# Other work in quarter units, on both sides of the probability products: a fused attention and long-convolution kernel

## The chip, the cores and the metric

The kernel runs on one core of a Trainium2 chip. The metric is device time in microseconds for one launch. Before the change the median of three runs is 1089.19 us (1088.64 to 1089.75).

## What is computed

Two independent layers on inputs of 2048 positions and 512 channels; their outputs stand side by side. The first is attention with 32 query heads of width 16 that share one key and one value head. The second is a gated long convolution, written with a Fourier transform.

```python
def _A_ref(x, wq, wk, wv, wo):            # x 1 x 2048 x 512, H = 32, Dh = 16
    q = (x @ wq).reshape(B, S, H, Dh).transpose(0, 2, 1, 3)
    k, v = x @ wk, x @ wv
    p = softmax(einsum("bhqd,bkd->bhqk", q, k) * Dh ** -0.5)
    o = einsum("bhqk,bkd->bhqd", p, v)
    return o.transpose(0, 2, 1, 3).reshape(B, S, H * Dh) @ wo

def _B_ref(q, k, v, shift_k, ssm_k, ssm_D):
    k_shift = causal convolution of k with shift_k, 4 taps
    kv = k_shift * v
    y = irfft(rfft(kv padded to 2 S) * rfft(ssm_k padded))[:S] + kv * ssm_D
    return q * y

out = concatenate([_A_ref(...), _B_ref(...)], axis=-1)
```

## The kernel before

**Attention.** A block is 512 queries of four heads, in two pairs, against 16 tiles of 128 keys. There are 32 such blocks (`NQ`) of 16 key tiles, two score tiles for each, so 1024 score tiles of 128 x 1024. For each of them TensorE makes two score matmuls (L699, `scores`), in float16 with 49 rows; ScalarE takes the exponential of the tile (L707); and TensorE multiplies half of the probabilities of two tiles with the values (L719, `pv`): four column-tiled products of 32 columns, 256 results wide, in float32, which stand as eight records in the trace. The value products of a block are summed in one PSUM bank, the accumulator (`self.acc`); at a block's end VectorE copies it out (L729).

**Turns.** `attend` (L735) writes the order out by hand. A turn issues three score tiles and their exponentials, then three value products of the turn before, then "other work" by `fill.step` (L755). If the accumulator changes inside a turn (`full`), the other work goes ahead of the first product of the new accumulator (L752). Three PSUM tiles hold scores, so the score matmul of a turn needs the exponential of the same place in the turn before. Two more banks (pool `pf`, L96) hold the accumulator and everything else that TensorE does: one bank for the other work at a time, besides the moments when the accumulator changes. 1024 score tiles in threes make 342 turns.

**Other work.** Six threads, Python generators, yield before each piece what it costs on TensorE and on VectorE:

- `rest_of_q` (L647): the query projection, 14 banks of 512 columns, each a sum of four products, cut by VectorE and stored; after each a bound for the softmax's shift (`bound`, L572); and at the end `flag` (L680), which reduces all bounds to one flag with a VectorE reduction, a TensorE transposition (L686) and two more VectorE operations.
- `conv_pe` (L388): the convolution's transforms. `forward` (L198, two products of 256 columns per bank, 16 banks for the short and 16 for the long transform of each of two channel blocks), `long_forward` with transposes ahead (L255), `backward` (L347, 16 banks of four products of 256 columns).
- `conv_short` (L413) and `conv_dve` (L429): VectorE alone, the four taps and the short Fourier steps and products between the transforms (L134 and others). `conv_pe` waits for them: the second `long` for the product of block 0, `backward` of a block for its inverse steps.
- `wo_heads` (L782) and `wo_part` (L816): the normalized heads come back from memory in 15 groups of which each needs a fixed step and some 15 steps of waiting, and a group's buffer (five of them) comes free when its projection is done. The output projection takes them in sets: groups 0 to 3, 4 to 7, 8 to 11, then 12 and 13, then 14, and the last block separately (L857 and `last`, L872).

`_Fill` (L894) hands them out. Each step adds a budget to two credits, TensorE's and VectorE's, capped (L919). Threads are asked in order; the one that `hurry` (L641) names comes first. A piece is issued when TensorE's credit covers it within a slack of 60, a VectorE piece while that credit is positive. Only one new piece per step, apart from those that continue the same bank (`HOLD`, the holder); while a bank is open no other thread may use TensorE. At the last turn `finish` (L945) issues whatever is left, ahead of the last value products.

A piece is a product 256 columns wide and costs 460 by the planner, a bound 350, a set of four transposes 500. A product (`mm`, L193) is four column-tiled matmuls, which become two passes with a weight load for each.

```python
RATE = 740.0, 2500.0        # added per turn: TensorE, VectorE
MOST = 1400.0, 2900.0       # caps
SLACK = 60.0
```

Of the kernel before, what the change touches and what calls it, by code (L numbers as in the profile page):

```python
# [39 lines left out]

RATE = 740.0, 2500.0
MOST = 1400.0, 2900.0
SLACK = 60.0
WO_AT = 290, 370, 440
OB = 5

# [34 lines left out]


WAIT = -1.0
HOLD = True


class _Emit:  # L90
# [18 lines left out]

    def wide(self):  # L110
        return self.ps.tile([P, 2, 512], F32, tag="s", name=self.nm("x"))

# [78 lines left out]
    def mm(self, out, w, x, start=True, stop=True):  # L193

        for j in range(0, P, 32):
            self.nc.tensor.matmul(out[j : j + 32], w[:, j : j + 32], x, start=start, stop=stop)  # L196

    def forward(self, src, c, m, ft):  # L198

        for q in range(2):  # L200
            yield (920 / 2, 700) if q else (920 / 2, 0, HOLD)
            if not q:
                b = self.bank()
            self.mm(b[:, q * CB : (q + 1) * CB], ft[:, q, :], src)
        self.nc.vector.tensor_copy(c[:, :, m, :], b.rearrange("p (q n) -> p q n", q=2))  # L205

    def table(self, n, m2):
        t = self.w.tile([P, 2, 2, P], F32, tag="ft", bufs=FT, name=self.nm(n))
# [6 lines left out]
    def conv_load(self):  # L215
        nc, I, w = self.nc, self.I, self.w
        self.dt = self.c.tile([P, 4], F32, name="dt")
        nc.sync.dma_start(self.dt, I["B_ssm_D"].rearrange("(c p) -> p c", p=P))
        sk = self.c.tile([P, 4, 4], F32, name="sk")
        nc.sync.dma_start(sk, I["B_shift_k"].rearrange("(c p) t -> p c t", p=P))  # L220
        yield WAIT, 6
        yield 240, 600
        tp = self.bank()
        for ct in range(4):
            nc.tensor.transpose(tp[0:4, ct * P : (ct + 1) * P], sk[:, ct, :], self.ident)
        tps = w.tile([4, 512], F32, tag="s2", bufs=S2, name="tps")
        nc.vector.tensor_copy(tps, tp[0:4, :])
        self.skd = self.dr.tile([4, 512], F32, name="skd")
        nc.sync.dma_start(self.skd, tps)
        rows = lambda t: t.rearrange("b (p m) c -> (b p) m c", m=16)  # L230
        self.kr, self.vr, self.qr, self.orr = rows(I["B_k"]), rows(I["B_v"]), rows(I["B_q"]), rows(self.out)
# [10 lines left out]
    def long_forward(self, blk, hin, ch):  # L242
# [14 lines left out]
            nc.vector.tensor_copy(hT[m], b.rearrange("p (i n) -> p i n", i=2))  # L257

        for m in (0, 2):
            yield 500, 700  # L260
            turn(m)
        for m in range(0, 16, 2):
            if m < 12:
                ft[m // 2 + 2] = self.table("ff", m // 2 + 2)
                yield 500, 700
                turn(m + 4)
            for i in range(2):
                yield from self.forward(hT[m][:, i, :], ch, m + i, ft[m // 2][:, i])
# [78 lines left out]
    def backward(self, blk, cx, places):  # L347
# [15 lines left out]
        for m2 in range(8):  # L363
            if m2 < 6:
                load(m2 + 2)
            if m2 == 7:
                self.seen.add(("b", blk))
            r = self.s2("r")
            for i in range(2):
                m = 2 * m2 + i  # L370
                for cc in range(2):
                    yield (920 / 2, 700) if i == cc == 1 else (920 / 2, 0, HOLD)
                    if i == cc == 0:
                        b = self.bank()
                    self.mm(
                        b[:, i * CB : (i + 1) * CB],
                        ft[m2][:, i, cc, :],
                        cx[:, cc, 4 * g2[m // 4] + g1[m % 4], :],
                        start=cc == 0,
                        stop=cc == 1,  # L380
                    )
            nc.vector.tensor_tensor(r, b.rearrange("p (i n) -> p i n", i=2), q[m2], ALU.mult)  # L382
            nc.gpsimd.dma_start(self.orr[:, 2 * m2 : 2 * m2 + 2, D + blk * CB : D + (blk + 1) * CB], r)  # L383

    def spectrum(self):
# [166 lines left out]
        nc.vector.tensor_scalar(self.wb[:, 8:16], blk[:, 0:8], cut, None, ALU.mult)  # L552
        nc.vector.tensor_scalar(self.gm[:, 16:17], kmr, cut, None, ALU.mult)

    def q_mm(self, g, c, b, dk, cols=slice(0, 512)):
        self.mm(b[:, cols], self.wq[g][:, dk, :], self.xT[c][:, dk, cols], start=dk == 0, stop=dk == 3)

    def q_out(self, g, c, b):

# [87 lines left out]
    def rest_of_q(self):  # L647
        for c in range(4):
            self.qc = c
            for g in range(4):  # L650
                if c == g == 0:
                    continue
                if c or g > 1:
                    b = None
                    for n in range(8):
                        yield (920 / 2, 0, HOLD) if n < 7 else (920 / 2, 2600)
                        b = b or self.bank()
                        self.q_mm(g, c, b, n % 4, slice(n // 4 * 256, n // 4 * 256 + 256))
                    self.q_out(g, c, b)
                yield WAIT, 2  # L660
                yield 350, 1100
                self.bound(g, c, self.bank())
            self.seen.add(f"q{c}")
            if c < 2:
                self.xT[c + 2] = self.w.tile([P, 4, 512], F32, tag="xt", bufs=2, name=f"xT{c + 2}")
                self.nc.sync.dma_start(self.xT[c + 2], self.xd[c])
        self.qc = 4
        self.flag()

    def stack(self, n, rows=KR):  # L670

# [8 lines left out]
    def flag(self):  # L680

        nc = self.nc
        g1 = self.c.tile([P, 1], F32, name="g1")
        nc.vector.tensor_reduce(g1, self.gm, AX.X, ALU.max)
        b = self.bank()
        nc.tensor.transpose(b[0:1, 0:P], g1, self.ident)  # L686
        g2 = self.c.tile([1, 1], F32, name="g2m")
# [47 lines left out]
    def attend(self, fill):  # L735
        self.od = self.dr.tile([NQ, P, 512], F32, name="od")
        x, steps = 0, NQ * NKT
        for u in range(3, 2 * steps + 3, 3):
# [7 lines left out]
            if u >= 2 * steps:  # L746
                fill.finish()

            full = [y for y in range(x + 1, end) if y % (2 * NKT) == 0]
            for y in range(x, end):  # L750
                if y in full:
                    fill.step(self.step)  # L752
                self.pv(y)
            if not full:
                fill.step(self.step)  # L755
            x = end
        self.last()

# [39 lines left out]

    def wo_rows(self, i, groups):

        b = None
        for h in range(2):
            cols = slice(256 * h, 256 * h + 256)
            for G in groups:
                yield (920 / 2, 700) if h and G == groups[-1] else (920 / 2, 0, HOLD)
                b = b or self.bank()
                self.mm(
                    b[:, cols],
                    self.oc[G][:, i * P : (i + 1) * P],
                    self.wo[G % 4][:, cols],  # L810
                    start=G == groups[0],
                    stop=G == groups[-1],
                )
        return b

    def wo_part(self):  # L816
        nc, w, I = self.nc, self.w, self.I
# [30 lines left out]
            yield 0, 1800  # L848
            self.over(self.ao, t, h)
        for i in range(4):  # L850
            b = yield from self.wo_rows(i, range(14, 15))
            nc.vector.tensor_tensor(self.wp[i], self.wp[i], b, ALU.add)
        for i in range(4):
            yield 920, 700
            b = self.bank()
            self.mm(b, t[:, 2, i * P : (i + 1) * P], self.wl[0])
            nc.vector.tensor_tensor(self.wp[i], self.wp[i], b, ALU.add)  # L857

    def over(self, a, t, h):

# [33 lines left out]
class _Fill:  # L894
# [3 lines left out]
    def __init__(self, threads, hurry):  # L898
# [2 lines left out]
        self.credit = [0.0, 0.0]  # L901
        self.holder = None

    def ask(self, t, i):

        while t[0] is not None and t[2] <= i:
            if t[1] is None:
                t[1] = next(t[0], None)
                if t[1] is None:
                    t[0] = None  # L910
                    return None
            if t[1][0] != WAIT:
                return t[1]
            t[2] = i + t[1][1]
            t[1] = None
        return None

    def step(self, i):
        c = self.credit = [min(c + r, m) for c, r, m in zip(self.credit, RATE, MOST)]  # L919
        once = True  # L920
        more = True
        while more:
            more = False
            first = self.hurry()
            for t in sorted(self.threads, key=lambda t: t is not self.threads[first or 0]):
                a = self.ask(t, i)
                if a is None:
                    continue
                if a[0] > 0:
                    if c[0] < a[0] - SLACK or not (once or self.holder is t) or self.holder not in (None, t):  # L930
                        continue
                    once = False
                    self.holder = t if len(a) > 2 else None
                elif c[1] <= 0:
                    continue
                c[0] -= a[0]
                c[1] -= a[1]
                t[1] = None
                t[1] = next(t[0], None)
                if t[1] is None:  # L940
                    t[0] = None
                more = True
                break

    def finish(self):  # L945
        while any(t[0] is not None for t in self.threads):
            for t in self.threads:
                if t[0] is None or self.holder not in (None, t):
                    continue
                if t[1] is None:  # L950
                    t[1] = next(t[0], None)
                if t[1] is None:
                    t[0] = self.holder = None
                else:
                    self.holder = t if len(t[1]) > 2 else None
                    t[1] = None
                    t[1] = next(t[0], None)
                    if t[1] is None:
                        t[0] = self.holder = None


def _general(tc, I, out):
# [149 lines left out]
```

## Time and profile before

| | us |
|---|---|
| median of three runs | 1089.19 |
| profiled execution | 1089.51 |
| its span, first to last instruction | 1087.7 |
| TensorE busy in matmuls | 1013.4 |
| ScalarE busy | 967.4 |
| VectorE busy | 610.4 |
| exponentials (L707), 1024 | 960.4 |
| value products (L719), 8192 records | 519.8 |
| score matmuls (L699), 2048 | 309.4 |

The mean granted clock of TensorE was 0.991. In the profile PE is TensorE's matmuls, PEld its weight loads (they overlap the matmuls), DVE is VectorE, ACT ScalarE, POOL GpSimd, SP SyncE; L196 is a line of the kernel, and since `mm` issues all products of the other work, they all stand under L196 and are told apart by their tiles (`f<-xT,wq` queries, `f<-a,ff`, `f<-hT,ff` and `f<-sp,fi` transforms, `f<-wo,o` and `f<-wl,lr` output projection). A group's row has its busy time, the mean duration of one in ns, then the idle time of the engine just before it and what ended that. A timeline row has its start, its duration (of a merged run of equal instructions), and in brackets the idle time before it. Matmul durations include the drain, which overlaps the next matmul, so costs are best read from start to start.

### The profile page before, as it was taken

What the parts mean: (1) busy time and instruction counts of PE and PEld (TensorE: products, weight loads), DVE (VectorE), ACT (ScalarE), POOL (GpSimd) and SP (SyncE); (2) the same over time, 40 slices, a digit from 0 to 9 for tenths busy, and PEclk for the clock granted to TensorE, in tenths of its full rate; (3) what the DMA queues carried; (4) which work ended last, traced back from release to release, by engine and by line L of the source; (5) the groups of instructions that cost most, each with busy time, mean ns of one, the idle gap of its engine ahead of it and who ended that gap; (6) DMA issues with size and microseconds to landing.
All of it is one profiled execution on the core that took longest, in us unless ns stands there. A gap on an engine that the chain in (4) does not pass through costs nothing.

```text
span 1087.7 us, 31787 instructions
## 1 busy us (share of the span) xinstructions
PE 1013.4 (93%) x13971; PEld 463.4 (43%) x13971; DVE 610.4 (56%) x825; ACT 967.4 (89%) x1032; POOL 96.3 (9%) x149
## 2 busy tenths in 40 slices
PE   7899999999999999999997999989988999998996
PEld 4344444444444444444443444434433444444442
DVE  3434774577577877786785356898789011000122
ACT  2798989999999999999997889999999999999993
POOL 2004210000000000013022021000000120000000
PEclk9899999999999999999999999999999999999999
DMA  6417433311211110113234243201011341110101
GB/s 218 147 48 229 131 136 140 102 53 56 110 54 44 54 54 26 43 57 125 63 119 131 84 139 117 70 29 39 29 49 40 97 136 41 38 39 28 49 2 42
DMA packets 47548, 87.30 MB, mean 80 GB/s; under 512 B 11132, under 2 KB 26026, under 8 KB 46380
## 3 DMA queue, kind: packets, MB, share of 16 engines
q1 hardware_dynamic: 33996, 43.50, 12.4%
q0 software_dynamic: 11648, 40.89, 11.6%
q8 instruction: 111, 1.82, 0.7%
q10 hardware_dynamic: 1760, 0.81, 0.3%
q14 instruction: 33, 0.27, 0.1%
HBM read 60.16 MB, written 25.02 MB: 78 GB/s over the span
## 4 chain that ended last, share of the span: by engine, by line
PE 66%; ACT 18%; issue 9%; DVE 4%; DMA 2%; POOL 0%; ACTq 0%; DVEq 0%; POOLq 0%
PE f L719 31%; PE s L699 18%; ACT p L707 18%; PE f L196 14%; PE f L255 1%; DMA xc<-in_A_x 1%; DMA kk<-in_B_k 1%; DVE ao L729 1%; DMA skd<-tps 1%; DMA wkv<-in_A_wk 1%; DVE t L312 0%; PE x L480 0%; DVE sp L134 0%; PE f L497 0%; DVE kc L515 0%
## 5 line engine op out<-in xcount | busy, mean ns | idle before, releaser
L707 ACT ACTIVATE p<-s 128x1024 f32<-128x1024 f32 x1024 | 960.4, 1069 | 84.3 <-PE s L699 76.7
L719 PE MATMUL f<-p,vx 128*32 128x256 f32 x8192 | 519.8, 385 | 5.4 <-DVE ao L729 5.3
L699 PE MATMUL s<-st,kst 49*128 49x512 f16 x2048 | 309.4, 382 | 41.4 <-ACT p L707 39.8
L719 PEld LDWEIGHTS f<-p,vx 128*32 128x32 f32 x8192 | 230.4, 110 | 234.1 <-issue 106.9
L699 PEld LDWEIGHTS <-kst 49*128 49x128 f16 x2048 | 97.3, 94 | 262.2 <-issue 219.2
L134 DVE TENSOR_TENSOR sp<-sp 128x1024 f32<-128x1024 f32 x96 | 111.6, 1213 | 0.0
L205 DVE COPY sp<-f 128x512 f32<-128x512 f32 x64 | 44.1, 689 | 76.0 <-PE f L196 75.7
L196 PE MATMUL f<-xT,wq 128*32 128x256 f32 (+1 forms) x960 | 67.8, 394 | 1.2 <-DVE gm L589 1.2
L729 DVE COPY ao<-f 128x512 f32<-128x512 f32 x31 | 21.4, 690 | 79.4 <-PE f L719 79.4
L196 PE MATMUL f<-wo,o 128*32 128x256 f32 x960 | 65.0, 379 | 0.0
L134 DVE TENSOR_TENSOR sp<-sp,sp 128x1024 f32<-128x1024 f32 x48 | 56.3, 1219 | 0.3
L824 DVE COPY wp<-f 128x512 f32<-128x512 f32 x12 | 8.3, 692 | 76.6 <-PE f L196 76.6
L382 DVE TENSOR_TENSOR r<-f,q 128x512 f32<-128x512 f32 x16 | 11.1, 692 | 65.7 <-PE f L196 65.7
L562 DVE TENSOR_SCALAR cut<-f 128x512 f32<-128x512 f32 x16 | 11.1, 691 | 64.2 <-PE f L196 64.0
L209 POOL DMA_DIRECT2D ff<-in_ff x32 | 17.6, 551 | 281.9 <-PE s L699 252.4
L196 PEld LDWEIGHTS f<-xT,wq 128*32 128x32 f32 x960 | 31.1, 110 | 23.3 <-issue 3.8
L196 PEld LDWEIGHTS f<-wo,o 128*32 128x32 f32 x960 | 31.2, 110 | 20.7 <-issue 0.2
L196 PE MATMUL f<-a,ff 128*32 128x256 f32 x512 | 34.5, 380 | 1.7 <-issue 0.9
L383 POOL DMA_DIRECT2D out<-r x16 | 11.6, 724 | 275.5 <-DVE r L382 252.0
L196 PE MATMUL f<-sp,fi 128*32 128x256 f32 x512 | 34.8, 379 | 0.0
L196 PE MATMUL f<-hT,ff 128*32 128x256 f32 x512 | 34.2, 379 | 0.0
L314 DVE TENSOR_TENSOR a<-a,t 128x512 f32<-128x512 f32 x48 | 33.1, 689 | 1.2
(106 smaller groups left out, 535.7 us busy)
## 6 DMA issues: line engine op xcount, KB each, us to landing
ff<-in_ff POOLq DMA_DIRECT2D x32, 256.0 KB, 4.2
od<-ao SPq DMA_DIRECT2D x30, 256.0 KB
kk<-in_B_k POOLq DMA_DIRECT2D x12, 640.0 KB, 4.7
qd<-qp SPq DMA_DIRECT2D x48, 128.0 KB
st<-qd SPq DMA_DIRECT2D x60, 98.0 KB
v<-in_B_v POOLq DMA_DIRECT2D x16, 256.0 KB, 4.5
hin<-in_B_ssm_k POOLq DMA_DIRECT2D x4, 1024.0 KB, 6.7
fi<-in_fi POOLq DMA_DIRECT2D x16, 256.0 KB, 3.8
```

The lines of the kernel that those rows point to most:

```text
L134: v.tensor_tensor(part(out), part(a), part(b), op)
L196: self.nc.tensor.matmul(out[j : j + 32], w[:, j : j + 32], x, start=start, stop=stop)
L205: self.nc.vector.tensor_copy(c[:, :, m, :], b.rearrange("p (q n) -> p q n", q=2))
L209: self.nc.gpsimd.dma_start(t, self.I[n][:, 2 * m2 : 2 * m2 + 2])
L314: nc.vector.tensor_tensor(a, a, t, ALU.add)
L382: nc.vector.tensor_tensor(r, b.rearrange("p (i n) -> p i n", i=2), q[m2], ALU.mult)
L383: nc.gpsimd.dma_start(self.orr[:, 2 * m2 : 2 * m2 + 2, D + blk * CB : D + (blk + 1) * CB], r)
L562: nc.vector.tensor_scalar(cut, b, LIM, -LIM, ALU.min, ALU.max)
L699: self.nc.tensor.matmul(s[:, e, :], self.kst[rows, k * P : (k + 1) * P], self.st[n][rows, pr, :], start=True, stop=True,)
L707: self.nc.scalar.activation(p, s, AF.Exp, scale=DH**-0.5 / SC / SC)
L719: nc.tensor.matmul(self.acc[32 * j : 32 * j + 32, cols], self.vx[:, k, :], self.pt[2 * i + j // 2][:, j % 2, cols], start=k == h == 0, sto ...
L729: nc.vector.tensor_copy(a, self.acc)
```

## The change

The unit of other work becomes a product's quarter, 128 columns, and both credits are counted in new sizes: 3 units a turn with a cap of 4, and 2300 for VectorE. A new generator `columns` offers what is left of a product and takes as many quarters as the credit covers, in one piece; pieces of different widths go into one bank, and only the first piece of a bank starts it. In a turn, `fill.turn` adds the budget; then, straight after the scores and ahead of the value products, `fill.step(self.step, False)` issues only pieces that continue an open bank; after the value products `fill.step(self.step, True)` may start a new bank, and issues VectorE's pieces. A turn with a change of accumulator has only the latter, at its old place. Transposes and bounds count two units and are not divided.

Products over 512 columns (queries, output projection) are no longer made in two halves of 256, but sum over the inner index with all 512 columns open. The projection of group 14 and of the block after it are summed in one bank and added once. `flag` is divided: the VectorE reduction first, five steps later the transposition. The slack is gone.

```diff
-RATE = 740.0, 2500.0
-MOST = 1400.0, 2900.0
-SLACK = 60.0
+RATE = 3.0, 2300.0
+MOST = 4.0, 2900.0
...
+    def columns(self, bank, first, w, x, last=False, dve=0):
+        n, k = 0, x.shape[-1] // P
+        while n < k:
+            g = yield k - n, dve, CONT if bank else NEW, PARTS
+            start = not bank
+            if start:
+                bank.append(self.bank())
+            c = slice(P * n, P * (n + g))
+            n += g
+            self.mm(bank[0][:, P * first + c.start : P * first + c.stop], w, x[:, c], start, last and n == k)
...
     def forward(self, src, c, m, ft):
+        b = []
         for q in range(2):
-            yield (920 / 2, 700) if q else (920 / 2, 0, HOLD)
-            if not q:
-                b = self.bank()
-            self.mm(b[:, q * CB : (q + 1) * CB], ft[:, q, :], src)
-        self.nc.vector.tensor_copy(c[:, :, m, :], b.rearrange("p (q n) -> p q n", q=2))
+            yield from self.columns(b, 2 * q, ft[:, q, :], src, q == 1, 700 * q)
+        self.nc.vector.tensor_copy(c[:, :, m, :], b[0].rearrange("p (q n) -> p q n", q=2))
...
-        self.flag()
+        yield from self.flag()
...
         g1 = self.c.tile([P, 1], F32, name="g1")
+        yield 0, 100
         nc.vector.tensor_reduce(g1, self.gm, AX.X, ALU.max)
+        yield WAIT, 5
+        yield 1, 200, NEW, WHOLE
         b = self.bank()
...
             full = [y for y in range(x + 1, end) if y % (2 * NKT) == 0]
+            fill.turn()
+            if not full:
+                fill.step(self.step, False)
             for y in range(x, end):
                 if y in full:
-                    fill.step(self.step)
+                    fill.step(self.step, True)
                 self.pv(y)
             if not full:
-                fill.step(self.step)
+                fill.step(self.step, True)
...
         for i in range(4):
-            b = yield from self.wo_rows(i, range(14, 15))
-            nc.vector.tensor_tensor(self.wp[i], self.wp[i], b, ALU.add)
-        for i in range(4):
-            yield 920, 700
-            b = self.bank()
-            self.mm(b, t[:, 2, i * P : (i + 1) * P], self.wl[0])
-            nc.vector.tensor_tensor(self.wp[i], self.wp[i], b, ALU.add)
+            b = []
+            yield from self.wo_row(b, i, 14, False)
+            yield from self.columns(b, 0, t[:, 2, i * P : (i + 1) * P], self.wl[0], True, 700)
+            nc.vector.tensor_tensor(self.wp[i], self.wp[i], b[0], ALU.add)
...
                 if a[0] > 0:
-                    if c[0] < a[0] - SLACK or not (once or self.holder is t) or self.holder not in (None, t):
+                    n = a[0] if a[3] == WHOLE else min(a[0], int(c[0]))
+                    if n < 1 or n > c[0] or not (once and new or self.holder is t) or self.holder not in (None, t):
                         continue
                     once = False
-                    self.holder = t if len(a) > 2 else None
-                elif c[1] <= 0:
+                elif c[1] <= 0 or not new:
                     continue
-                c[0] -= a[0]
-                c[1] -= a[1]
+                c[0] -= n
+                c[1] -= a[1] if n == a[0] else 0
+                self.give(t, n)
```

`backward`, the queries and the output projection use `columns` in the same way.

More of the change, by code (lines that the diff above doesn't have):

```diff
@@ L86 @@
 WAIT = -1.0
-HOLD = True
+NEW, CONT = 0, 1
+WHOLE, PARTS = 0, 1
 class _Emit:
@@ L221, in conv_load @@
         yield WAIT, 6
-        yield 240, 600
+        yield 1, 600, NEW, WHOLE
         tp = self.bank()
@@ L259, in long_forward @@
         for m in (0, 2):
-            yield 500, 700
+            yield 2, 700, NEW, WHOLE
             turn(m)
@@ L264, in long_forward @@
                 ft[m // 2 + 2] = self.table("ff", m // 2 + 2)
-                yield 500, 700
+                yield 2, 700, NEW, WHOLE
                 turn(m + 4)
@@ L371, in backward @@
                 for cc in range(2):
-                    yield (920 / 2, 700) if i == cc == 1 else (920 / 2, 0, HOLD)
-                    if i == cc == 0:
-                        b = self.bank()
[L375 to L382, printed above, removed]
+                    x = cx[:, cc, 4 * g2[m // 4] + g1[m % 4], :]
+                    last = i == cc == 1
+                    yield from self.columns(b, 2 * i, ft[m2][:, i, cc, :], x, last, 700 * last)
+            nc.vector.tensor_tensor(r, b[0].rearrange("p (i n) -> p i n", i=2), q[m2], ALU.mult)
             nc.gpsimd.dma_start(self.orr[:, 2 * m2 : 2 * m2 + 2, D + blk * CB : D + (blk + 1) * CB], r)
@@ L553, in k_max, with q_mm @@
         nc.vector.tensor_scalar(self.gm[:, 16:17], kmr, cut, None, ALU.mult)
-    def q_mm(self, g, c, b, dk, cols=slice(0, 512)):
-        self.mm(b[:, cols], self.wq[g][:, dk, :], self.xT[c][:, dk, cols], start=dk == 0, stop=dk == 3)
+    def q_mm(self, g, c, b, dk):
+        self.mm(b, self.wq[g][:, dk, :], self.xT[c][:, dk, :], start=dk == 0, stop=dk == 3)
     def q_out(self, g, c, b):
@@ L653, in rest_of_q @@
                 if c or g > 1:
[L654 to L659, printed above, removed]
+                    b = []
+                    for dk in range(4):
+                        w, x = self.wq[g][:, dk, :], self.xT[c][:, dk, :]
+                        yield from self.columns(b, 0, w, x, dk == 3, 2600 * (dk == 3))
+                    self.q_out(g, c, b[0])
                 yield WAIT, 2
-                yield 350, 1100
+                yield 2, 1100, NEW, WHOLE
                 self.bound(g, c, self.bank())
@@ L799, in wo_rows, with wo_row @@
     def wo_rows(self, i, groups):
[L801 to L814, printed above, removed]
+        b = []
+        for G in groups:
+            yield from self.wo_row(b, i, G, G == groups[-1])
+        return b[0]
+    def wo_row(self, b, i, G, last):
+        x = self.oc[G][:, i * P : (i + 1) * P]
+        yield from self.columns(b, 0, x, self.wo[G % 4], last, 700 * last)
     def wo_part(self):
@@ L850, in wo_part @@
         for i in range(4):
-            b = yield from self.wo_rows(i, range(14, 15))
-            nc.vector.tensor_tensor(self.wp[i], self.wp[i], b, ALU.add)
-        for i in range(4):
-            yield 920, 700
-            b = self.bank()
-            self.mm(b, t[:, 2, i * P : (i + 1) * P], self.wl[0])
-            nc.vector.tensor_tensor(self.wp[i], self.wp[i], b, ALU.add)
+            b = []
+            yield from self.wo_row(b, i, 14, False)
+            yield from self.columns(b, 0, t[:, 2, i * P : (i + 1) * P], self.wl[0], True, 700)
+            nc.vector.tensor_tensor(self.wp[i], self.wp[i], b[0], ALU.add)
     def over(self, a, t, h):
@@ L902, in __init__, with go @@
         self.holder = None
+    def go(self, t, x):
+        try:
+            t[1] = t[0].send(x)
+        except StopIteration:
+            t[0] = t[1] = None
     def ask(self, t, i):
@@ L907, in ask, with give, turn, step @@
             if t[1] is None:
[L908 to L912, printed above, removed]
+                self.go(t, None)
+            elif t[1][0] == WAIT:
+                t[2] = i + t[1][1]
+                t[1] = None
+            else:
                 return t[1]
-            t[2] = i + t[1][1]
-            t[1] = None
-        return None
-    def step(self, i):
-        c = self.credit = [min(c + r, m) for c, r, m in zip(self.credit, RATE, MOST)]
-        once = True
+        return None
+    def give(self, t, n):
+        self.go(t, n or None)
+        if n:
+            self.holder = t if t[1] is not None and len(t[1]) > 2 and t[1][2] == CONT else None
+    def turn(self):
+        self.credit = [min(c + r, m) for c, r, m in zip(self.credit, RATE, MOST)]
+    def step(self, i, new):
+        c, once = self.credit, True
         more = True
@@ L928, in step @@
                     continue
+                n = 0
                 if a[0] > 0:
-                    if c[0] < a[0] - SLACK or not (once or self.holder is t) or self.holder not in (None, t):
+                    n = a[0] if a[3] == WHOLE else min(a[0], int(c[0]))
+                    if n < 1 or n > c[0] or not (once and new or self.holder is t) or self.holder not in (None, t):
                         continue
                     once = False
-                    self.holder = t if len(a) > 2 else None
-                elif c[1] <= 0:
+                elif c[1] <= 0 or not new:
                     continue
-                c[0] -= a[0]
-                c[1] -= a[1]
[L938 to L941, printed above, removed]
+                c[0] -= n
+                c[1] -= a[1] if n == a[0] else 0
+                self.give(t, n)
                 more = True
@@ L947, in finish @@
             for t in self.threads:
[L948 to L959, printed above, removed]
+                if t[1] is None or t[1][0] == WAIT:
+                    if t[0] is not None:
+                        self.go(t, None)
+                elif self.holder in (None, t):
+                    self.give(t, t[1][0])
 def _general(tc, I, out):
```

## The prediction

> **What bounds the kernel now.** I read the page's groups first, then the timeline of TensorE in a stretch without other work and in one with it, then the long waits.
>
> ```profile
> span 1087.7 us, 31787 instructions
> PE 1013.4 (93%) x13971; PEld 463.4 (43%) x13971; DVE 610.4 (56%) x825; ACT 967.4 (89%) x1032; POOL 96.3 (9%) x149
> ...
> L707 ACT ACTIVATE p<-s 128x1024 f32<-128x1024 f32 x1024 | 960.4, 1069 | 84.3 <-PE s L699 76.7
> L719 PE MATMUL f<-p,vx 128*32 128x256 f32 x8192 | 519.8, 385 | 5.4 <-DVE ao L729 5.3
> L699 PE MATMUL s<-st,kst 49*128 49x512 f16 x2048 | 309.4, 382 | 41.4 <-ACT p L707 39.8
> ...
> L134 DVE TENSOR_TENSOR sp<-sp 128x1024 f32<-128x1024 f32 x96 | 111.6, 1213 | 0.0
> ```
>
> The 1024 exponentials of ScalarE are issued three to a turn, so there are 342 turns. ScalarE waits 76.7 us for scores, and TensorE waits 39.8 us for exponentials: the two take turns at being late. The timeline shows what a turn costs. Without other work:
>
> ```profile
> 1028.50 0.39 PE L699 MATMUL s<-st,kst 49*128 49x512 f16 x2 [0.52 <-ACT p L707]
> ...
> 1031.25 0.39 PE L699 MATMUL s<-st,kst 49*128 49x512 f16 x2 [0.39 <-ACT p L707]
> ```
>
> From third score to third score is 2.75 us, with TensorE waiting in each: ScalarE alone sets this, 0.92 us per exponential. With other work (L196; eight matmul records are one product with 128 x 256 results, which I call a half, so two of the change's quarters):
>
> ```profile
> 540.40 0.82 PE L699 MATMUL s<-st,kst 49*128 49x512 f16 x6
> ...
> 543.45 0.82 PE L699 MATMUL s<-st,kst 49*128 49x512 f16 x6
> 544.20 1.50 PE L719 MATMUL f<-p,vx 128*32 128x256 f32 x24
> 545.52 0.61 PE L196 MATMUL f<-sp,fi 128*32 128x256 f32 x8
> 546.07 0.60 PE L699 MATMUL s<-st,kst 49*128 49x512 f16 x4
> 546.85 0.39 PE L699 MATMUL s<-st,kst 49*128 49x512 f16 x2 [0.18 <-ACT p L707]
> 547.17 1.50 PE L719 MATMUL f<-p,vx 128*32 128x256 f32 x24
> 548.49 1.05 PE L196 MATMUL f<-sp,fi 128*32 128x256 f32 x16
> 549.47 0.82 PE L699 MATMUL s<-st,kst 49*128 49x512 f16 x6
> ```
>
> A turn with two halves after another such takes 3.05 us (540.40 to 543.45), one with one half 2.62, so a half costs 0.43 and the bare turn of TensorE is 2.19. The 2.62 is shorter than ScalarE's 2.75: TensorE runs ahead, the next turn's third score must wait for an exponential (546.85, where 546.51 would have done: unhindered, the third score stands 0.44 after the first, 0.82 less its own 0.38), the two halves come on top, and that turn takes 3.40. The pair costs 6.02 us where ScalarE needs 5.50 and TensorE 5.67. The old credits give one, two, one, two, two halves in five turns (8 x 460 = 3680 of 5 x 740): 2 x 6.02 + 3.05 = 15.09 us for 16 quarters, where five bare turns are 13.75. So a quarter of other work costs 1.34 / 16 = 84 ns of span.
>
> **Evenness.** A three-quarter turn is 2.62 + 0.215 = 2.83 us for TensorE, over ScalarE's 2.75. Is it free of the third score's wait? In the rows above the waiting third score began 3.40 after its predecessor turn's start (543.45 to 546.85), so in the next turn it stands no earlier than 3.40 after the start, and unhindered at turn length plus 0.44. A turn of length L therefore makes the next one 3.40 - 0.44 - L = 2.96 - L longer: after 2.83 comes 2.96, after 2.96 again 2.83. The mean is 2.895, so a quarter costs (2.895 - 2.75) / 3 = 48 ns instead of 84. All turns at 2.83 would make it 27, all at 2.96 it would be 70.
>
> How many quarters? By the code: queries 14 x 16 = 224, six transforms of 64 = 384, output projection 3 x 64 + 32 + 32 = 256, so 864. I went through the planner's rules turn by turn, credits and waits included. For the kernel before this gives just the empty stretches that the trace has:
>
> ```profile
> 694.00:743.00 49.00, 0.00 (x0) 0.00 (x0) 1.00 0.15 46
> 806.00:849.00 43.00, 0.00 (x0) 0.00 (x0) 1.00 0.11 33
> ```
>
> (L196's busy time in two windows; two shorter ones follow.) With the new rules and rates, 3 quarters a turn instead of 3.2, the work is spread out: one empty stretch of 33 turns is left (about turns 256 to 288, waiting for the inverse transform on VectorE, which gets 2300 a turn instead of 2500), and 832 quarters are done by the last turn. Gain: 832 x 36 ns = 30 us; ends 832 x 14 = 12 and 832 x 57 = 47. I take 30, as the alternation of 2.83 and 2.96 follows from the waiting row.
>
> **The tail.** The price of the slower rate: by my count the projection of heads 12 and 13 ends in turn 341 of 342, and its last 32 quarters (four rows of output, two products of 512 columns each) are issued all at once by the finish, before the last two probability products. Before, two products of 512 were left there.
>
> ```profile
> 1070.21 1.04 PE L196 MATMUL f<-wl,lr 128*32 128x512 f32 x8
> 1072.07 1.07 PE L196 MATMUL f<-wl,lr 128*32 128x512 f32 x8 [0.81 <-DVE wp L857]
> ```
> ```profile
> L864 DVE STREAM_TRANSPOSE lr<-ao x2: 439/439/439, 1042.6 to 1044.7; 128x256 f32<-128x256 f32 x2
> L870 DVE TENSOR_TENSOR lr<-ao,lr x2: 424/425/426, 1044.3 to 1046.4; 128x256 f32<-128x256 f32 x2
> L864 DVE STREAM_TRANSPOSE lr<-f x2: 440/444/449, 1074.1 to 1076.1; 128x256 f32<-128x256 f32 x2
> L870 DVE TENSOR_TENSOR lr<-f,lr x2: 424/424/425, 1075.8 to 1077.9; 128x256 f32<-128x256 f32 x2
> ```
>
> A product of 512 columns costs 0.86, and with one bank free beside the accumulator the next row's bank waits for VectorE: 1.86 from start to start, so 1.0 for the copy. The normalization of the heads before (L864 to L870, both halves) takes 1042.6 to 1046.8, 4.2 us of VectorE, and would now run in turn 341 ahead of the first row's addition. From that turn's score matmul, at 0: three quarters and the products to 2.3, row 0's first product to 3.1, its second after half of the normalization, at 4.0 to 4.9; its addition only after the other half, 6.1 to 6.8; then three rows of 1.73 with two waits of 1.0 between, to 14.0; two products 0.86, so the last normalization begins at about 15.0. Before, that turn began at 1068.6 (one score, 0.31, and three products, 1.32, ahead of 1070.21) and the last normalization at 1074.1, so 5.5. Cost: 9.5 us, with ends 6 (normalization a turn earlier) and 13.
>
> **The flag.** The maximum over the queries' bounds is now reduced on VectorE five steps before TensorE transposes it.
>
> ```profile
> 589.00 0.82 PE L699 MATMUL s<-st,kst 49*128 49x512 f16 x6
> ...
> 596.42 0.37 PE L686 MATMUL f<-ident,g 128*1 128x128 f32 x1 [5.40 <-DVE g L684]
> ...
> 602.43 0.82 PE L699 MATMUL s<-st,kst 49*128 49x512 f16 x6
> ```
> ```profile
> 582.50:602.00 19.50, 13.63 (x166) 5.62 (x167) 12.65 (x23) 12.12 (x13) 6.32 (x9) 0.82 0.57 186
> ```
>
> TensorE stands 5.4 us there, with the granted clock at 0.82 over the stretch; two turns take 13.4 instead of about 6.0. Gain 7.4, ends 5.4 and 8.
>
> **Banks.** A bank that a continuing piece completes ahead of the probabilities is followed, after them, by a new one in the same turn; before, a whole turn's scores lay between as well. By the count this happens 54 times. VectorE must empty the bank meanwhile:
>
> ```profile
> 543.58 0.69 DVE L382 TENSOR_TENSOR r<-f,q 128x512 f32<-128x512 f32 x1 [2.36 <-PE f L196]
> ```
>
> The two halves from 542.47 on stream until 543.33, the evacuation ends 0.94 later. Three probability products cover 1.32 (1.50 with the drain), so 0.38 is spare. One 1.21 us operation (L134) just begun on VectorE would exceed it by 0.8. Ends 0 and 54 x 0.5 = 27; VectorE mostly idles before an evacuation, as this row's 2.36 us show, so I take 54 x 0.08 = 4. At the 31 changes of accumulator the other work still goes before the new accumulator, but as at most 3 quarters (0.65) where two halves covered 0.86 of the 0.94: 0.2 x some 20 of them, 4, ends 0 and 6.
>
> **Narrow pieces.** 184 pieces are a single quarter, 128 columns.
>
> ```profile
> 500.08 0.35 PEld L196 LDWEIGHTS f<-hT,ff 128*32 128x32 f32 x8
> ```
> ```profile
> 229.90 0.71 PE L255 MATMUL f<-ident,hin 128*128 128x128 f32 x4
> ...
> 232.87 0.38 PE L255 MATMUL f<-ident,hin 128*128 128x128 f32 x1
> ```
>
> Each product is two passes, and the loads of both take 0.35 with 0.22 between them, so 0.13 for the four of one pass; a 128-column pass streams for 0.11. If loads hide behind the pass before, a pass takes at most 0.13 and a quarter 0.26 instead of 0.215; if they don't, 0.48. The transposes of 128 columns speak for hiding: three more take 0.33, 0.11 each, with a weight load for each. I take 2 us for all, ends 0 and 38 (next part). The total number of pieces hardly grows, as 512-column operands go in pieces of up to four quarters: 472 with the finish, against 432.
>
> **Sum** against the profiled execution (1089.5 us, of which 1087.7 are the span): -30 - 7.4 + 9.5 + 4 + 4 + 2 = -18, so 1071.6; the median of the runs shown is 0.3 lower: **1071 us**.
>
> **Rivals.**
> (1) Narrow pieces are bound by their loads, and the kernel gets slower. At 0.48 a quarter, a turn with one single has 3.10 us of TensorE work, over 2.96, so it takes 3.10 instead of 2.895: 184 x 0.205 = 38 us, 1107. It decides from about 0.38 us a piece, where 184 x 0.10 eats the 18. For it: 0.13 of loads is more than 0.11 of streaming. Against it: the transposes. Chance 0.06. A milder form: a narrow pass costs half as much again, so a quarter 0.31; the turn becomes 2.93, the mean with 2.96 is 2.94, 184 x 0.05 = 9 us, 1078. Chance 0.12. Here the Trainium skill's page "TensorE: Matmul & The Clock Gate", section "Back-to-back issue gap", speaks against the change: in a stream of load and matmul pairs it gives about 81 ns per 128-column matmul, against about 56 for an isolated one, so about half as much again. No run here has narrow column-tiled products yet, so that rule is open.
> (2) VectorE is late at the 54 changes by 0.5 us each: 27 instead of 4, 1094. For it: VectorE is at work 56% of the span, much of it in 1.2 us pieces; against it, the 2.36 us of idling. Chance 0.06.
> (3) The third score waits in every turn with work, all take 2.96, and the evenness is worth 12 instead of 30: 1089, no change. For it: TensorE's 2.83 is only 0.08 over ScalarE's 2.75, and any small delay of an exponential shows. Chance 0.10, of which 0.04 ends just on the faster side.
>
> **How the numbers follow.** The forecast has 0.66. What a measurement can tell from no change is about 0.2%, 2 us. Faster: 0.66 + 0.12 + 0.04 = 0.82; same 0.06; slower 0.06 + 0.06 = 0.12. The range: downwards all turns at 2.83 (-17), so 1054; upwards to the milder rival 1 and most of rival 3, so 1088; rival 1's hard form and rival 2 lie outside.
>
> **What would show it.** In the changed kernel's timeline, turns with three quarters should take 2.83 and 2.96 by turns, and 3.40 be gone; TensorE's 5.4 us before the transposition of the flag should be gone; the other work should leave one long gap, and eight products of 512 columns should stand together before the end, with waits for VectorE of about 1 us. A single quarter between two others should move the next start by about 0.22. I am wrong if narrow pieces take 0.3 or more, if new waits of TensorE for VectorE add up to over 10 us ahead of the tail, or if turns with work stay near 3.0 on average.

## The result and the profile after

The changed kernel takes 1064.38 us (median of four runs, 1063.43 to 1064.7) where the kernel before takes 1089.26 on the same chip: a ratio of 0.977, 95% interval 0.9754 to 0.9787. That is 24.9 us; the prediction's sum was 18. The profiled execution is one of 1063.43 us, with a span of 1061.7.

From the page after, the span, the engines' busy shares and the groups that answer to those shown of before (`scores` stands at L707 now, the exponential at L715, `pv` at L727):

```profile
span 1061.7 us, 32477 instructions
...
PE 1010.3 (95%) x14315; PEld 472.4 (44%) x14315; DVE 607.6 (57%) x821; ACT 973.1 (92%) x1032; POOL 95.9 (9%) x149
...
L715 ACT ACTIVATE p<-s 128x1024 f32<-128x1024 f32 x1024 | 966.1, 1057 | 43.4 <-PE s L707 26.3
L727 PE MATMUL f<-p,vx 128*32 128x256 f32 x8192 | 512.6, 381 | 6.7 <-DVE ao L737 6.7
...
L707 PE MATMUL s<-st,kst 49*128 49x512 f16 x2048 | 309.2, 382 | 21.6 <-ACT p L715 19.4
```

No engine's work became shorter by more than 0.5%. What shrank is their mutual waiting, ScalarE's for scores from 76.7 to 26.3 us, TensorE's for exponentials from 39.8 to 19.4. The timeline of TensorE late in the kernel shows how. Each score group of six records opens a turn:

```profile
1004.16 0.95 PE L707 MATMUL s<-st,kst 49*128 49x512 f16 x6
1005.04 0.42 PE L196 MATMUL f<-sp,fi 128*32 128x128 f32 x8
1005.28 1.48 PE L727 MATMUL f<-p,vx 128*32 128x256 f32 x24
1006.58 0.61 PE L196 MATMUL f<-wo,o 128*32 128x256 f32 x8
1007.13 0.83 PE L707 MATMUL s<-st,kst 49*128 49x512 f16 x6
1007.88 0.86 PE L196 MATMUL f<-wo,o 128*32 128x256 f32 x16
1008.56 1.48 PE L727 MATMUL f<-p,vx 128*32 128x256 f32 x24
1009.97 0.95 PE L707 MATMUL s<-st,kst 49*128 49x512 f16 x6
1010.84 0.85 PE L196 MATMUL f<-wo,o 128*32 128x384 f32 x8
```

The turns take 2.97 and 2.84, and the score group takes 0.95 or 0.83: in every second turn the third score waits 0.12 for its exponential. (A wait as short as this shows only as a longer score group; the 19.4 above does not contain it.) The turn of 3.40 is gone as a rhythm. In the first turn one quarter completes a bank ahead of the value products and two open the next behind them; in the second, pieces of 256 and of 128 columns continue it (merged into one row of 16 records); in the third 384 columns are one piece.

The other work leaves one gap, where before there were four (L196's busy time in a window inside it):

```profile
792.00:880.00 88.00, 0.00 (x0) 0.00 (x0) 1.00 0.13 39
```

And it runs to the very end, where eight products of 512 columns pile up between the last score and the last value products:

```profile
1033.18 0.39 PE L707 MATMUL s<-st,kst 49*128 49x512 f16 x2
1033.49 0.85 PE L196 MATMUL f<-wo,o 128*32 128x384 f32 x8
1034.16 1.48 PE L727 MATMUL f<-p,vx 128*32 128x256 f32 x24
1035.46 1.04 PE L196 MATMUL f<-wo,o 128*32 128x512 f32 x8
1037.27 1.06 PE L196 MATMUL f<-wl,lr 128*32 128x512 f32 x8 [0.77 <-issue]
1039.90 1.07 PE L196 MATMUL f<-wo,o 128*32 128x512 f32 x8 [1.56 <-DVE wp L860]
1040.78 1.04 PE L196 MATMUL f<-wl,lr 128*32 128x512 f32 x8
1042.63 1.07 PE L196 MATMUL f<-wo,o 128*32 128x512 f32 x8 [0.81 <-DVE wp L860]
...
1047.11 1.05 PE L727 MATMUL f<-p,vx 128*32 128x256 f32 x16
```

From the last turn's single score to the end of the span are 28.5 us, before 19.1 (from 1068.6). So the turns ahead of it gave 35.4 (the last turn begins at 1033.2 instead of 1068.6), and the end took 9.4 back.

### The profile page after: what moved, and what is told of

The parts are those of the page before. It is cut to its first block, busy times and chain, and to the rows that moved or that the text cites. A ratio compares the mean times of both kernels' runs of the same rounds, so it can differ in the third digit from the quotient of the medians.

```text
span 1061.7 us, 32477 instructions
## 1 busy us (share of the span) xinstructions
PE 1010.3 (95%) x14315; PEld 472.4 (44%) x14315; DVE 607.6 (57%) x821; ACT 973.1 (92%) x1032; POOL 95.9 (9%) x149
## 4 chain that ended last, share of the span: by engine, by line
PE 77%; ACT 9%; DVE 7%; issue 5%; DMA 1%; ACTq 0%; DVEq 0%
PE f L727 35%; PE s L707 22%; PE f L196 18%; ACT p L715 9%; DVE ao L737 1%; DVE sp L134 1%; PE f L267 1%; DMA wkv<-in_A_wk 1%; DMA xc<-in_A_x 1%; DVE sp L217 0%; PE x L486 0%; PE f L503 0%; DVE u L183 0%; DVE kc L521 0%; DVE sp L185 0%
## 5 line engine op out<-in xcount | busy, mean ns | idle before, releaser
L715 ACT ACTIVATE p<-s 128x1024 f32<-128x1024 f32 x1024 | 966.1, 1057 | 43.4 <-PE s L707 26.3
L727 PE MATMUL f<-p,vx 128*32 128x256 f32 x8192 | 512.6, 381 | 6.7 <-DVE ao L737 6.7
L727 PEld LDWEIGHTS f<-p,vx 128*32 128x32 f32 x8192 | 248.9, 110 | 200.4 <-issue 59.8
L707 PE MATMUL s<-st,kst 49*128 49x512 f16 x2048 | 309.2, 382 | 21.6 <-ACT p L715 19.4
L707 PEld LDWEIGHTS <-kst 49*128 49x128 f16 x2048 | 102.0, 94 | 251.2 <-issue 197.1
L196 PE MATMUL f<-wo,o 128*32 128x128 f32 (+3 forms) x920 | 69.6, 396 | 3.2 <-DVE wp L860 3.2
L196 PE MATMUL f<-xT,wq 128*32 128x128 f32 (+3 forms) x880 | 71.2, 421 | 0.2 <-DVE gm L595 0.2
L196 PE MATMUL f<-hT,ff 128*32 128x256 f32 (+1 forms) x648 | 38.7, 338 | 0.5 <-DVE sp L217 0.5
L196 PE MATMUL f<-a,ff 128*32 128x128 f32 (+1 forms) x672 | 39.1, 332 | 0.0
L196 PE MATMUL f<-sp,fi 128*32 128x256 f32 (+1 forms) x680 | 38.3, 331 | 0.0
L196 PEld LDWEIGHTS f<-wo,o 128*32 128x32 f32 x920 | 22.3, 109 | 27.6 <-issue 15.8
L324 DVE TENSOR_TENSOR t<-kk,tpb 128x512 f32<-128x512 f32 x48 | 32.8, 683 | 0.0
```

The source lines that it names most:

```text
L324: nc.vector.tensor_tensor(t, kx(i), tap(i), ALU.mult)
L707: self.nc.tensor.matmul(s[:, e, :], self.kst[rows, k * P : (k + 1) * P], self.st[n][rows, pr, :], start=True, stop=True,)
L715: self.nc.scalar.activation(p, s, AF.Exp, scale=DH**-0.5 / SC / SC)
L727: nc.tensor.matmul(self.acc[32 * j : 32 * j + 32, cols], self.vx[:, k, :], self.pt[2 * i + j // 2][:, j % 2, cols], start=k == h == 0, sto ...
```

## The experiments

Each was run beside the kernel before on the same chip; ratios are to that, with 95% intervals. My theory was that the gain is the fit: every turn with work brings TensorE just over ScalarE's time. The rivals were the order (continuing pieces ahead of the value products), the lower rate, and the flag.

**The sizes alone undone.** Order, rates and flag of the change, but pieces of two or four quarters:

```diff
-                    n = a[0] if a[3] == WHOLE else min(a[0], int(c[0]))
+                    n = a[0] if a[3] == WHOLE else min(a[0], int(c[0])) // 2 * 2
```

> The changed kernel, but a piece is two or four quarters, never one or three; order and rates are the same, so turns alternate between one half and two. If the evenness is the gain, pairs cost 6.02 us instead of 5.80 again: by the count of turns some 23 us more, and 44 quarters instead of 32 left at the end, 3 to 5 us: about 1091. If the order or the lower rate is the gain: 1064 to 1069.

Measured 1090.64, ratio 1.0015 (1.0006 to 1.0025): the whole gain is gone, as the first expectation said. TensorE's timeline has the old pair again:

```profile
542.37 0.82 PE L707 MATMUL s<-st,kst 49*128 49x512 f16 x6
...
544.99 0.60 PE L707 MATMUL s<-st,kst 49*128 49x512 f16 x4
545.77 0.39 PE L707 MATMUL s<-st,kst 49*128 49x512 f16 x2 [0.18 <-ACT p L715]
...
548.39 0.82 PE L707 MATMUL s<-st,kst 49*128 49x512 f16 x6
```

One half, 2.62 us, then two, 3.40: 6.02, though the halves now stand on both sides of the value products. The last turn begins at 1054.0 instead of 1033.2, so the odd quarters are worth 21 us in the turns and some 5 at the end. Order, rates and flag alone bring nothing net. They do bring something in the turns: without odd quarters the last turn still begins 14.6 earlier than in the kernel before (1068.6), with 40 quarters fewer done by then. But the end, 33.3 instead of 19.1, takes all of it back.

**The rate alone.** The kernel before with `RATE = 690.0, 2300.0`, which is three quarters a turn in halves.

> The kernel before, still in halves and behind the value products, with both budgets of the change: 690 a turn, which is three quarters, and 2300. If the lower rate alone is the gain: about 1070. If evenness is, a pair of turns still costs 6.02 us for six quarters; the turns gain about 6 by the count, and some 34 quarters are left for the end, about 10: about 1093.

Measured 1099.71, ratio 1.0096 (1.0079 to 1.0113). The rate alone loses. The last turn begins at 1055.6, so the turns gained 13 rather than 6; 5.0 of that are the flag's two turns, which take 8.4 here for 13.4, since the new order leaves TensorE 1.7 us to wait there instead of 5.4. But the end takes 41.9 us instead of 19.1, much longer than counted. A window over it shows why:

```profile
1055.60:1097.50 41.90, 25.24 (x206) 6.80 (x202) 15.09 (x35) 2.13 (x4) 0.00 (x0) 0.66 0.08 27
```

TensorE was busy for 25.24 of 41.90, and the granted clock was 0.66. It waits there, and from its longest wait on (3.67 us for VectorE, until 1063.8) a product of 512 columns takes 1.94 instead of 1.05. Such a pile is dearer than its products. This one also has eight additions to wait for, where the change, which sums group 14 and the last block in one bank, has four; no run separates that from the rate. In the changed kernel's pile the clock held (1.00 from 1035.5 to 1048.0).

**The order.** The change with the first step moved behind the value products, so that pieces, rates and counts stay:

```diff
             fill.turn()
-            if not full:
-                fill.step(self.step, False)
             for y in range(x, end):
...
             if not full:
+                fill.step(self.step, False)
                 fill.step(self.step, True)
```

> The changed kernel, but the pieces that continue a bank are issued behind the value products too, directly ahead of a new bank; pieces, rates and counts are the same. If the place ahead of the products is what covers the emptying of a bank, each of the 54 changes of bank within a turn now costs TensorE about 1.0 us: some 50 us, about 1115. If VectorE is early enough or only the even size counts: about 1064.

Measured 1120.93, ratio 1.0291 (1.0274 to 1.0308): 56 us slower than the change, near the first expectation. The longest waits of TensorE are the banks':

```profile
PE f L196 <- DVE sp L217: 20.3, 25, 0.8
...
PE f L196 <- DVE r L388: 7.3, 9, 0.8
```

Each wait is 0.8 us, nearly the 0.94 that an evacuation takes. So the three value products between two banks do hide it, and the place ahead of them is what makes pieces smaller than a bank affordable: a condition of the gain, not a gain.

**Narrow pieces.** Every piece a single quarter, 832 pieces in the turns instead of 463:

```diff
-                    n = a[0] if a[3] == WHOLE else min(a[0], int(c[0]))
+                    n = a[0] if a[3] == WHOLE else min(1, int(c[0]))
```

> The changed kernel, but every piece is a single quarter: some 830 pieces instead of 464 in the turns, three to a turn. If loads hide behind the pass before, a narrow piece costs some 0.02 us over its share, a three-quarter turn 2.90 instead of 2.84, its mean with 2.96 is 2.93: about 1070. If a turn is bound by the number of matmuls that are issued, 54 instead of 46 or fewer at some 62 ns, a turn takes 3.35: about 1180. If narrow passes wait for their loads at 0.48 a quarter, a turn takes 3.6: over 1250.

Measured 1065.18, ratio 0.978 (0.9764 to 0.9796), 0.8 more than the change; the intervals overlap. The timeline has three singles in a row (24 records):

```profile
970.78 0.82 PE L707 MATMUL s<-st,kst 49*128 49x512 f16 x6
971.53 0.86 PE L196 MATMUL f<-sp,fi 128*32 128x128 f32 x24
972.21 1.48 PE L727 MATMUL f<-p,vx 128*32 128x256 f32 x24
973.62 0.95 PE L707 MATMUL s<-st,kst 49*128 49x512 f16 x6
```

They take 0.86, where one piece of 384 columns took 0.85 above, and the turn 2.84. Here the loads hide, with three times as many of them.

**Four quarters a turn.** As even, but further over ScalarE's time: `RATE = 4.0, 2300.0`.

> The changed kernel with four units a turn instead of three: as even, but a turn with work is 3.05 us of TensorE against 2.75 of ScalarE, and the third score never waits. If what counts is that TensorE stays just over ScalarE's time, a quarter costs 75 ns instead of 48 to 60: some 25 us more in the turns, and some 9 less at the end, where only 4 quarters are left: about 1080. If evenness alone counts, the turns cost the same and the end is better: about 1055.

Measured 1068.36, ratio 0.9805 (0.9788 to 0.9821): 4.0 more than the change, between the two expectations.

```profile
304.52 0.82 PE L707 MATMUL s<-st,kst 49*128 49x512 f16 x6
305.27 1.06 PE L196 MATMUL f<-xT,wq 128*32 128x512 f32 x8
306.15 1.48 PE L727 MATMUL f<-p,vx 128*32 128x256 f32 x24
307.56 0.82 PE L707 MATMUL s<-st,kst 49*128 49x512 f16 x6
```

In a run of work the turns are 3.05 and no score waits, as expected. The last turn begins 15.6 later than in the change, not 25, and the end is 10.5 shorter. Both parts have the expected sign: a turn further over ScalarE's time costs more, and an emptier end gives back. The turns with work do cost about as much more as I had counted: their excess over 2.75 is 75.3 us for 812 quarters, 28 more than in the change. What I had left out is the other turns, which are 13 shorter together. Of these, 4.6 are the turns without work: there are 86 of them instead of 33, and 11, each right behind a run of work, take 2.19, as in the kernel before.

**A shorter end.** The change with four units a turn from step 470 of 512 on:

```diff
-            fill.turn()
+            fill.turn(self.step)
...
-    def turn(self):
-        self.credit = [min(c + r, m) for c, r, m in zip(self.credit, RATE, MOST)]
+    def turn(self, i):
+        rate = RATE if i < 470 else (4.0, 2300.0)
+        self.credit = [min(c + r, m) for c, r, m in zip(self.credit, rate, MOST)]
```

> The changed kernel with four units a turn from step 470 of 512 on, so that 8 quarters instead of 32 are left for the finish. If the pile at the end costs 9.4 us, of which two products as before cost nothing, the end gains 9 and some 29 turns cost 4 more: about 1060. If the end is set by the heads' last waits and normalization instead, it only loses the 4: about 1068.

Measured 1057.66, ratio 0.9708 (0.9692 to 0.9724): the fastest version, 6.7 under the change.

```profile
1036.79 0.39 PE L707 MATMUL s<-st,kst 49*128 49x512 f16 x2
1037.11 1.06 PE L196 MATMUL f<-wl,lr 128*32 128x512 f32 x8
1037.99 1.48 PE L727 MATMUL f<-p,vx 128*32 128x256 f32 x24
1039.29 1.04 PE L196 MATMUL f<-wo,o 128*32 128x512 f32 x8
1040.15 1.04 PE L196 MATMUL f<-wl,lr 128*32 128x512 f32 x8
1041.01 1.05 PE L727 MATMUL f<-p,vx 128*32 128x256 f32 x16
```

The last turn begins 3.6 later, the end takes 18.5 instead of 28.5. The pile was the cost of the end.

**The flag.** First alone in the kernel before:

```diff
-        self.flag()
+        yield from self.flag()
...
+        yield 0, 100
         nc.vector.tensor_reduce(g1, self.gm, AX.X, ALU.max)
+        yield WAIT, 5
+        yield 240, 200
         b = self.bank()
```

> The kernel before, with the flag alone divided as in the change: reduction, five steps of waiting, then the transposition. If the two turns at the flag cost 13.4 us for 6.0, as read in the trace of before, it gains 7.4 us: about 1082. If only TensorE's 5.4 us of idling go, and the slow clock behind it is not the flag's: about 1084. If the wait only moves to the change of accumulator that lies in the same turn: about 1089.

Measured 1084.58, ratio 0.9951 (0.9934 to 0.9967): 4.8, not 7.4. The time is near the second expectation, but not by its mechanism: part of the wait has moved to the accumulator, as the third said. At its place TensorE now waits for the accumulator's emptying, which stands behind four operations in VectorE's queue, and the clock falls after that (second fence: the window's clock is 0.83):

```profile
590.35 0.38 PE L576 MATMUL f<-qa,wb 128*32 128x512 bf16 x1
592.72 0.64 PE L722 MATMUL f<-p,vx 128*32 128x256 f32 x8 [1.99 <-DVE ao L732]
593.30 0.82 PE L702 MATMUL s<-st,kst 49*128 49x512 f16 x6
...
597.98 0.82 PE L702 MATMUL s<-st,kst 49*128 49x512 f16 x6
```
```profile
588.00:598.00 10.00, 8.01 (x95) 3.12 (x89) 9.05 (x15) 6.72 (x8) 4.00 (x6) 0.83 0.58 180
```

Two turns still take 9.3 instead of 6.0. Then the change with the flag undivided:

```diff
-        yield from self.flag()
+        self.flag()
...
-        yield 0, 100
         nc.vector.tensor_reduce(g1, self.gm, AX.X, ALU.max)
-        yield WAIT, 5
-        yield 1, 200, NEW, WHOLE
```

> The changed kernel with the flag undivided, as before: the reduction, the transposition at once and the two operations behind it, in the turn of the last bound. If the flag's own wait is what cost in the kernel before, TensorE stands some 4 to 6 us and its clock falls for as long again: 1069 to 1072. If it was the change of accumulator in the same turn and VectorE's queue of that place, which the new order has moved apart, it costs 1 to 2: about 1066.

Measured 1062.81 (1061.58 to 1064.88), ratio 0.9761 (0.9744 to 0.9777): not slower than the change. TensorE's wait at that place is small, 1.7 us instead of 5.4, but in the profiled execution the clock falls behind it (second fence: 0.82):

```profile
690.44 1.04 PE L704 MATMUL s<-st,kst 49*128 49x512 f16 x6
...
694.77 0.27 PE L691 MATMUL f<-ident,g 128*1 128x128 f32 x1 [1.66 <-DVE g L689]
694.97 0.82 PE L704 MATMUL s<-st,kst 49*128 49x512 f16 x6
...
699.59 0.90 PE L704 MATMUL s<-st,kst 49*128 49x512 f16 x6
```
```profile
690.40:699.60 9.20, 7.49 (x84) 3.11 (x82) 3.19 (x8) 6.24 (x7) 0.00 (x0) 0.82 0.16 46
```

These two turns take 9.15, where the change takes 6.02 in the turns with the last bound (690.18 to 696.20). In this trace the last turn begins 3.7 later than in the change, and the end is 2.3 shorter. This execution took 1064.88, with a mean clock of 0.993; another of the four took 1061.58, with 0.998. So in the change the division of the flag takes away a stall of some 3 us of that trace, and the median over executions shows no gain from it. The new order had already moved the flag away from the crowded change of accumulator.

**VectorE's budget.** The kernel before with 2300 instead of 2500:

> The kernel before, with VectorE's budget at 2300 a turn instead of 2500 and nothing else. If the smaller budget takes away the few late emptyings of the accumulator (three turns with some 1.5 us each): about 1084. If it only makes VectorE's chain longer and leaves some 4 more quarters than before for the end: about 1091.

Measured 1087.99, ratio 0.9985 (0.9975 to 0.9994): 1.4 us, between the two: its turns are 4.9 shorter, and its end, with 8 more quarters left, is 3.7 longer. Of the three turns with late emptyings two are short again, but one elsewhere grew from 3.62 to 4.85. The changed kernel with 2500 instead of 2300:

> The changed kernel with VectorE's budget at 2500 instead of 2300. If the budget matters through late emptyings, now with less cover: about 1072. If it hardly matters, the count of turns gives some 3 us more in the turns and 3 quarters less at the end: about 1066.

Measured 1070.51, ratio 0.9826 (0.9809 to 0.9842), 6.1 more than the change. It is near the first expectation, but for another reason; the emptyings of the accumulator wait no longer than in the change (6.5 us against 6.7). In the order that the larger budget brings, TensorE waits for a table once:

```profile
654.01 1.48 PE L727 MATMUL f<-p,vx 128*32 128x256 f32 x24
660.36 0.66 PE L196 MATMUL f<-a,ff 128*32 128x128 f32 x8 [4.87 <-DMA ff<-in_ff]
660.95 1.46 PE L707 MATMUL s<-st,kst 49*128 49x512 f16 x6
```

The score group behind the wait takes 1.46 instead of 0.82: the clock has fallen. The two turns there take 13.2 us instead of 5.8, which is more than the difference.

## Why the prediction was right, and where its terms were not

- **Evenness**, forecast 30. Its mechanism stood: the turns alternate between 2.84 and 2.97, as the prediction's waiting row gave (2.83 and 2.96), and undoing the odd quarters takes back everything net. The size was off: 21 us in the turns by the halves' experiment. The mis-sized step is the price of a quarter, on both sides. 48 ns holds inside the rhythm; over all 255 turns with work apart from changes of accumulator, transposes and bounds, the excess over 2.75 is 47.3 us for 780 quarters, 61 ns, mostly because 23 turns that start a run have four quarters, take 3.04 to 4.06 and hold 12.9 of it. Counted in the same way, the kernel before has 78.5 us for 806 quarters, 97 ns instead of the prediction's 84: ten of its turns start a run with six quarters, take 3.59 to 4.07 and hold 11.5, and three others take 4.5 to 4.7. Both prices were 13 too low, so their difference of 36 ns came out by luck. And not all of it is evenness: the halves' run, with the order, rates and flag of the change, has 69.0 us for 760 quarters, 91 ns, so the odd quarters are worth 30 ns each.
- **Count of turns.** The trace has what the count gave: the gap in turns 256 to 288, 184 pieces of one quarter (1472 matmul records of 128 columns), 32 quarters left.
- **The tail**, forecast 9.5, measured 9.4. The last normalization begins 15.0 us after that turn's score, at 1048.2, as worked out; before it was 5.5.
- **The flag**, forecast 7.4: 4.8 alone, and within the change some 3 in one trace and nothing in the medians. The step that failed is "two turns take 13.4 instead of about 6.0": it put the whole stretch down to the flag, but 2.0 us of idling with the clock behind it belong to the accumulator's emptying in the same turn.
- **Banks and accumulators**, forecast 4 and 4. TensorE's waits for a bank of the transforms are 1.1 us in all in the change's list of waits, so the spare 0.38 us held. The waits for the accumulator went from 5.3 to 6.7.
- **Narrow pieces**, forecast 2: at most 1, as 369 more of them cost 0.8.
- **What was not foreseen.** In the turns the change gained 8 more than forecast, with evenness 9 under it. The flag alone and the evenness make 26 of the 35.4. Of the remaining 9, some 2 are the 27 further quarters that moved out of the turns to the end (at 84 ns each). Some turns with late emptyings, of 4.3 to 5.0 us before, have no counterpart in the change; but no experiment isolates them, and the budget's two runs show that they come and go with any shift of the order. The lower rate may have a part in it, as it made 8 us outside the flag's turns in the kernel before, with 28 quarters fewer. This part stays open.

The three rivals lost. Narrow pieces cost their columns and no more; here the rule of the Trainium skill's page "TensorE: Matmul & The Clock Gate", section "Back-to-back issue gap" (some 81 ns for a 128-column matmul in a stream, half as much again as alone) does not carry over, since three singles took 0.86 against 0.85 for one piece of 384 columns. VectorE was not late. And the third score waited in every second turn, not in all.

## What to carry to other kernels

When two engines take turns at the limit with little buffering between them, price the filler by the turn, not by the sum: work that pushes one turn under the other engine's time and the next one over it costs both shortfalls. Choose a unit small enough that each turn lands just over the other engine's time, and put pieces that finish a buffer where other work covers its emptying. Then look at the end: a rate that fits the middle can leave a pile for the finish, and a faster rate for the last turns was worth as much as a quarter of the whole change.

## What the hardware showed that I had not expected

- A turn of three single quarters issues 54 matmuls and as many weight loads in 2.84 us, 53 ns for a matmul, and no longer than a turn with fewer, wider pieces (1007.13 to 1009.97 in the change), so their number sets no limit here.
- An idle stretch of TensorE of only 1.99 us was followed by a granted clock of 0.83 over 10 us. Products then take nearly twice as long (24 records of value products 2.79 instead of 1.50), so by estimate that is half the clock for some 3.4 us; the 5.4 us of the kernel before had 0.82 over 19.5, some 7 us of half clock. Such a stall costs its own length and, by the same estimate, 1.7 and 3.5 us more. But the length alone does not decide: behind the undivided flag, 1.66 us were enough in the change (0.82 over 9.2 us), while in the kernel before with the lower rate 1.67 at the same operation left the clock at 1.00 (448.0 to 458.0), and in the kernel before 1.76 for the accumulator left the clock at 1.00 (629.0 to 639.0). What decides is not shown.
- At the end of the kernel before with the lower rate, with TensorE busy for 60% of 41.9 us, the clock was 0.66. It fell behind a wait of 3.67 us and stayed down through six waits of 0.8 to 0.9. In the change's pile three such waits and one of 1.56 left it at 1.00: there short waits alone did not bring it down.
